# An attention and MLP backward kernel bound by its DMA: head 0's scores ahead of the output-gradient columns, the first loads reordered, dx sums and a weight load moved forward

## The chip, the cores and the metric

The kernel runs on one core of one Trainium2 chip. The metric is device time in microseconds (us), the median over executions. A core has a matrix engine (PE; its weight loads are listed as PEld), a vector engine (DVE), a scalar engine (ACT), GpSimd (POOL) and SyncE (SP, which here issues loads and, at the very end, two tiny stores). In the timelines below each engine takes its instructions in the order in which the program lists them, so that one whose inputs are ready can stand behind others. The profile counts sixteen DMA engines; a DMA share of 1.00 means that all sixteen are busy.

## The reference, cut to what matters

The result is the output of a gated mix of one attention step and one MLP, and the gradients of nine inputs. There is one query token, 32 heads, a K and a V cache of 4096 x 128 bf16 (1 MB each) per head, and a model width of 640.

```python
def _fwd_reference(A_x, A_k_cache, A_v_cache, A_wq, A_wo, B_x, B_w1, B_b1, B_w2, gate_w):
    x = A_x                                           # (1, 1, 640)
    g = _sigmoid((x * gate_w).sum(-1, keepdims=True))
    a = _A_ref(x, A_k_cache, A_v_cache, A_wq, A_wo)   # q = x@wq; softmax(q.K)V; @ wo
    b = _B_ref(B_x, B_w1, B_b1, B_w2)                 # 640 -> 1728 -> 640
    return g * a + (1 - g) * b

def reference(..., grad_out):
    _out, _vjp = jax.vjp(_f, A_x, A_k_cache, A_v_cache, A_wq, A_wo, B_w1, B_b1, B_w2, gate_w)
    return (_out, *_vjp(grad_out))
```

For each head the kernel reads K and V and writes gradients dK and dV of the same size: 32 heads times four tiles of 1024 KB are 134 MB of the 164.93 MB that it moves. The weights and their gradients are the rest.

## The kernel before

Everything is unrolled in Python. Heads come in groups of four (G = 4). One load of Wq serves eight heads (1280 KB), one load of Wo four (640 KB). All large loads go through SP's queue, in this order at the start:

```python
vec_rows = const.tile([3 * RC, P], BF16, name="vec_rows")
nc.scalar.dma_start(vec_rows[0:RC, :], x_rows)            # three tiny loads, by ACT
nc.scalar.dma_start(vec_rows[RC:2 * RC, :], dy_rows)
nc.scalar.dma_start(vec_rows[2 * RC:3 * RC, :], gw_rows)
...
load_wq(0); load_wo(0); load_k(0); load_v(0); load_k(1); load_v(1); load_wo(1)
# w1_sb, b1c
load_k(2); load_v(2)
load_w2(0); load_w2(1)         # two tiles w2c of 96 partitions x 7680 bytes, 720 KB each
```

Gradients dK and dV go out by GpSimd's queue as each head ends. `products` are matrix-vector products on transposed chunks of K or V; `qd` holds the columns of q and of the output gradient that they are multiplied with. These columns are prepared group by group. Small pieces of work (`steps`) wait in a list, and `slot` issues those whose inputs were issued in an earlier slot:

```python
add(n("qcol"), "P", qcol, (), head)                       # q = Wq x, needs the Wq load
add(n("doa"), "D", do_part(0, 2), (), head)               # output gradient, needs Wo
add(n("dob"), "D", do_part(2, 4), (n("doa"),), head)
add(n("qbc"), "P", qbc, (n("qcol"),), head)
add(n("dbc"), "P", dbc, (n("dob"), n("qbc")), head)
add(n("dcol"), "P", dcol, (n("dbc"),), head)
add(n("m2"), "T", m2, (n("dcol"),), head)                 # columns of q AND gradient
add(n("x2"), "P", x2, (n("m2"),), head)
```

```python
prep_steps(0, 0)
for _ in range(8):
    slot(0, 9, 9)              # all of head 0's columns first
tk = []
for c in range(NT):            # then head 0's scores
    k_chunk(0, c, tk)
    if c:
        s_chunk(0, c - 1, tk)
s_chunk(0, NT - 1, tk)
mlp_steps()
for h in range(H):
    hh, g = h % G, h // G
    if hh == 3:
        load_wo(g + 2)
        if g % 2 == 0:
            load_wq(g // 2 + 1)      # reuses the tile that the dx sums read
    load_k(h + 3)
    load_v(h + 3)
    if hh == 1 and g + 1 < NG:
        rest = steps[:]
        steps.clear()
        prep_steps(g + 1, h)         # the next group's columns go first
        steps.extend(rest)
    ...
    period(h)                        # softmax, dP, dV, dq, next head's scores, store of dV
```

(Cuts are marked by dots; assertions are left out.)

## Time and profile before

| | before |
|---|---|
| median, range (first 3 runs) | 413.43 us, 413.16 to 413.49 |
| span of the profiled run | 412.1 us |
| moved by DMA | 164.93 MB, mean 400 GB/s |
| busy: DVE, PE, ACT | 75%, 74%, 43% |
| first store of dV issued | 29.66 us |

A kernel that moves 164.93 MB at the 421 GB/s of most of its span needs 392 us, so about 20 us are to be found where the rate is lower. The page's second part cuts the span into 40 equal slices. Its line DMA gives the mean busy share of the sixteen engines in tenths; the line GB/s gives what they moved. Before:

```profile
DMA  8999999999999999999999999999999999999970
GB/s 292 421 405 336 421 425 415 421 423 425 420 426 422 423 411 415 424 421 422 427 411 425 423 421 419 420 424 393 407 401 428 422 422 421 422 423 383 421 313 14
DMA packets 26328, 164.93 MB, mean 400 GB/s; under 512 B 2812, under 2 KB 2812, under 8 KB 10012
```

The slice that reads 336 (30.9 to 41.2 us) is remarkable: the engines are as busy as elsewhere and move less. The view of windows gives, for each stretch, its start, end and length in us, then busy us and number of instructions of PE, PEld, DVE, ACT and POOL, then the granted PE clock, the DMA share and GB/s. Before:

```profile
0.00:4.00 4.00, 0.00 (x0) 0.00 (x0) 1.45 (x7) 1.28 (x1) 0.94 (x11) 1.00 0.46 134
4.00:16.00 12.00, 3.73 (x40) 2.64 (x40) 5.41 (x22) 2.18 (x7) 0.00 (x0) 1.00 1.02 407
30.00:36.00 6.00, 5.01 (x112) 4.62 (x110) 4.48 (x11) 3.24 (x8) 0.85 (x2) 1.00 1.01 244
30.00:40.00 10.00, 7.74 (x142) 6.95 (x141) 7.88 (x19) 4.57 (x11) 0.93 (x3) 0.92 1.01 315
270.00:290.00 20.00, 13.82 (x251) 12.64 (x252) 12.56 (x32) 7.18 (x17) 1.59 (x3) 0.73 0.99 406
400.00:407.00 7.00, 0.00 (x0) 0.00 (x0) 0.00 (x0) 0.00 (x0) 0.00 (x0) 0.50 0.06 26
```

From 30 to 36 us the rate is 244 GB/s at a DMA share of 1.01: this is "the dip" from here on. What ran there is in the DMA view of 30 to 35 us, before (queue, packets, MB, share of the sixteen engines; q1 carries the loads that SP issues, q0 the transfers that GpSimd issues):

```profile
DMA packets 179, 1.23 MB, mean 245 GB/s; under 512 B 21, under 2 KB 21, under 8 KB 172
## 3 DMA queue, kind: packets, MB, share of 16 engines
q1 hardware_dynamic: 178, 1.21, 100.0%
```

Only loads are in flight, and nearly all their packets are under 8 KB: these are the 7680-byte rows of w2c. They take 503 ns each here (median of the packet records of the two tiles), but 291 ns at 208 to 226 us, where stores run beside the same sort of load. Loads without stores are not slow as such: just before, K and V load alone (99% of the engines' time) at 415 GB/s and 309 ns for an 8 KB packet:

```profile
26.00:29.00 3.00, 2.47 (x45) 2.12 (x42) 2.68 (x7) 1.21 (x3) 0.00 (x0) 1.00 0.99 415
```

Nor is it the row of 7680 bytes alone: the six 8 KB packets that start at 30 to 35 us take 456 to 541 ns too. So every load packet beside w2c is slow while no store runs; what makes it so is not shown. No store runs at 30 to 35 us because the first one has only just been issued, as the timeline of before shows (start, length, engine, line, operation, in brackets how long the engine had been idle and what ended it):

```profile
6.74 0.17 PE L180 MATMUL cols_ps<-ident_bf,vec_rows 15*128 15x15 bf16 x1 [6.74 <-DMA vec_rows<-in_gate_w_dram]
11.25 0.67 PE L269 MATMUL qc_ps<-cols_bf,wq_g 128*128 128x1 bf16 x20
16.77 1.95 PE L559 MATMUL tr<-ident_f,Kn 128*128 128x128 f32 x8
22.29 0.19 DVE L632 TENSOR_REDUCE m<-sA 128x1 f32<-128x32 f32 x1 [5.60 <-PE sA L568]
29.66 0.67 POOL L611 DMA_DIRECT2D out_dram<-dV_sb  x1 [28.10 <-DVE o_all L673]
```

The tiny vectors land at 6.7 us, q is made at 11.25, the transposes of K0 start at 16.77 after the gradient columns, the scores end on PE at 22.25, and the store of dV is issued at 29.66. At the end of the kernel, 26 GB/s from 400 to 407 us is one sixteenth of 421: one engine finishes late.

### The profile page before, as it was taken

The page shows a single profiled execution, that of the slowest core. Times are in us where ns is not written, and L with a number is a line of the kernel's source. Part 1 is how long each engine was busy: PE and PEld are TensorE (multiplying, and loading weights), DVE is VectorE, ACT ScalarE, POOL GpSimd, SP SyncE. Part 2 cuts the span into 40 slices and gives each one's busy share as a digit, 9 for nine tenths or more (in the row PEclk, how much of TensorE's full clock was granted, in tenths as well). Part 3 has the DMA queues.
Part 4 walks back from the last instruction along what each step waited for, and adds up shares of the span by engine and source line. Part 5 has one row for each costly group of instructions (what it writes and reads, how often), then busy time and mean ns, then how long its engine had stood idle before and what let it go on. Part 6 is the DMA issues. An engine that isn't in the chain of part 4 may idle for free.

```text
span 412.1 us, 13687 instructions
## 1 busy us (share of the span) xinstructions
PE 305.7 (74%) x5916; PEld 277.5 (67%) x5916; DVE 308.8 (75%) x807; ACT 177.0 (43%) x410; POOL 49.9 (12%) x95
## 2 busy tenths in 40 slices
PE   0688899988998789898977688439888788886200
PEld 0577888888887678787867687428777678775200
DVE  3338655685679999999897688528999997978840
ACT  1354534434445455445534356305554555543000
POOL 0001001111110111121111112001111111133310
PEclk9998999999999999989996899958999999999555
DMA  8999999999999999999999999999999999999970
GB/s 292 421 405 336 421 425 415 421 423 425 420 426 422 423 411 415 424 421 422 427 411 425 423 421 419 420 424 393 407 401 428 422 422 421 422 423 383 421 313 14
DMA packets 26328, 164.93 MB, mean 400 GB/s; under 512 B 2812, under 2 KB 2812, under 8 KB 10012
## 3 DMA queue, kind: packets, MB, share of 16 engines
q1 hardware_dynamic: 14116, 82.03, 48.8%
q0 software_dynamic: 12112, 82.03, 47.8%
q8 instruction: 46, 0.75, 0.7%
q14 instruction: 14, 0.11, 0.1%
q10 hardware_dynamic: 40, 0.01, 0.0%
HBM read 82.03 MB, written 82.03 MB: 398 GB/s over the span
## 4 chain that ended last, share of the span: by engine, by line
DVE 33%; PE 30%; DMA 23%; ACT 7%; issue 3%; ACTq 0%; DVEq 0%
DMA Kn<-in_A_k_cache_dram 17%; PE tr L559 10%; DVE dK_sb L584 8%; DVE dV_sb L584 7%; DMA out_dram<-dK_sb 6%; ACT tT L561 6%; PE sA L628 4%; DVE junk L376 4%; PE sA L568 3%; PE h_ps L407 3%; PE sB L681 3%; DVE junk L279 2%; DVE junk L508 2%; PE sB L568 1%; DMA vec_rows<-in_gate_w_dram 1%
## 5 line engine op out<-in xcount | busy, mean ns | idle before, releaser
L561 ACT COPY tT<-tr 128x512 f32<-128x512 f32 x256 | 142.3, 587 | 140.9 <-PE tr L559 140.2
L568 PEld LDWEIGHTS <-tT 128*128 128x128 bf16 x2048 | 80.4, 98 | 40.3 <-ACT tT L561 34.9
L559 PE MATMUL tr<-ident_f,Kn 128*128 128x128 f32 x512 | 80.7, 295 | 6.5 <-DMA Kn<-in_A_k_cache_dram 6.5
L584 DVE TENSOR_TENSOR dV_sb<-p_bf,qd 128x2048 bf16<-128x2048 bf16 x64 | 77.9, 1218 | 2.8 <-DMA out_dram<-dK_sb 2.8
L584 DVE TENSOR_TENSOR dK_sb<-ds_bf,qd 128x2048 bf16<-128x2048 bf16 x64 | 77.7, 1215 | 0.0
L559 PE MATMUL tr<-ident_f,Vn 128*128 128x128 f32 x512 | 72.6, 277 | 0.1
L568 PE MATMUL sA<-qd,tT 128*128 128x48 bf16 x1024 | 48.8, 187 | 23.5 <-ACT dq_all L686 12.8
L559 PEld LDWEIGHTS tr<-ident_f,Kn 128*128 128x128 f32 x512 | 60.1, 150 | 7.6 <-issue 6.2
L559 PEld LDWEIGHTS tr<-ident_f,Vn 128*128 128x128 f32 x512 | 56.8, 143 | 0.2 <-PE sA L568 0.2
L568 PE MATMUL sB<-qd,tT 128*128 128x48 bf16 x1024 | 46.1, 183 | 0.1
L611 POOL DMA_DIRECT2D out_dram<-dV_sb x32 | 18.3, 572 | 166.8 <-DVE dV_sb L584 74.2
L628 PEld LDWEIGHTS <-Vn 128*128 128x128 bf16 x1024 | 30.2, 96 | 10.4 <-issue 10.4
L601 POOL DMA_DIRECT2D out_dram<-dK_sb x31 | 18.3, 591 | 151.0 <-DVE rz L650 77.7
L628 PE MATMUL sA<-e_bf,Vn 128*128 128x48 bf16 x1024 | 30.7, 183 | 7.6 <-DVE zs L648 6.0
L681 PE MATMUL sB<-ds_bf,Kn 128*128 128x48 bf16 x1024 | 31.8, 185 | 3.5 <-DVE ds_bf L670 3.5
L681 PEld LDWEIGHTS <-Kn 128*128 128x128 bf16 x1024 | 29.2, 97 | 3.8 <-issue 3.8
L632 DVE TENSOR_REDUCE m<-sA 128x1 f32<-128x32 f32 x32 | 6.0, 189 | 31.3 <-PE sA L568 25.6
L279 DVE SCALAR_TENSOR_TENSOR junk<-wo_g,da_bc 128x640 bf16<-128x640 bf16 x32 | 26.3, 821 | 2.6 <-ACT da_bc L220 1.1
L376 DVE SCALAR_TENSOR_TENSOR junk<-wq_g,dq_bc 128x1024 bf16<-128x1024 bf16 (+1 forms) x25 | 25.1, 1004 | 0.2
L668 DVE TENSOR_SCALAR_CACHE_REDUCE dj<-sB,rz 128x128 f32<-128x128 f32 x32 | 11.1, 346 | 11.2 <-PE sB L662 11.2
L407 PE MATMUL h_ps<-cols_bf,w_sb 128*96 128x1 bf16 x90 | 18.2, 313 | 1.4 <-ACT qd L290 0.7
L407 PEld LDWEIGHTS <-w_sb 128*96 128x96 bf16 x90 | 17.6, 272 | 1.8 <-issue 0.7
(144 smaller groups left out, 283.8 us busy)
## 6 DMA issues: line engine op xcount, KB each, us to landing
Kn<-in_A_k_cache_dram SPq DMA_DIRECT2D x32, 1024.0 KB, 27.2
Vn<-in_A_v_cache_dram SPq DMA_DIRECT2D x32, 1024.0 KB, 26.9
out_dram<-dV_sb POOLq DMA_DIRECT2D x32, 1024.0 KB, 12.2
out_dram<-dK_sb POOLq DMA_DIRECT2D x31, 1024.0 KB, 12.3
wq_g<-in_A_wq_dram SPq DMA_DIRECT2D x4, 1280.0 KB, 19.0
wo_g<-in_A_wo_dram SPq DMA_DIRECT2D x8, 640.0 KB, 13.3
out_dram<-wo_g POOLq DMA_DIRECT2D x8, 640.0 KB, 11.6
out_dram<-dwq_t POOLq DMA_DIRECT2D x5, 896.0 KB, 16.6
```

The costliest lines, as they stand in the source:

```text
L279: nc.vector.scalar_tensor_tensor(junk[:, 0:D], in0=wos[g][:, i, :], scalar=1.0, in1=da_bc[:], op0=ALU.mult, op1=ALU.mult, accum_out=gp["do ...
L376: nc.vector.scalar_tensor_tensor(junk[:, c0:c1], in0=wqs[w][:, rc, c0:c1], scalar=1.0, in1=dq_bc[:, w * WG * Dh + c0:w * WG * Dh + c1], op ...
L407: nc.tensor.matmul(hps[a][:, fc:fc + 1], lhsT=w1_sb[:, rc, :].rearrange("p (q c) -> p q c", c=FCN)[:, :, fc], rhs=x_bf[:, rc:rc + 1], star ...
L559: nc.tensor.transpose(tp[:, t, :], flat[:, k * P:(k + 1) * P], ident_f[:])
L561: nc.scalar.copy(sb[:].rearrange("p a b -> p (a b)"), tp[:].rearrange("p a b -> p (a b)"))
L568: nc.tensor.matmul(out[:, 2 * k:2 * k + W], lhsT=tb[:, t, par, :], rhs=vec[:, par, :].unsqueeze(1).to_broadcast([P, W // 2, 2]), start=(pa ...
L584: nc.vector.tensor_tensor(dst[:, a:b, :].rearrange("p j (a b) -> p j a b", b=2), col[:, a:b, :].unsqueeze(2).to_broadcast([P, n, Dh // 2, 2]),
L601: nc.gpsimd.dma_start(dKv[h], st["dK"][:])
L611: nc.gpsimd.dma_start(dVv[h], st["dV"][:])
L628: nc.tensor.matmul(O, lhsT=vts[h][:, j, :], rhs=st["e"][:, j:j + 1].to_broadcast([P, W]), start=(j == 0), stop=(j == J - 1))
L668: nc.vector.tensor_scalar(dj[:], PT, rz[:], None, ALU.mult, ALU.add, accum_out=dd[:])
L681: nc.tensor.matmul(DQ, lhsT=kts[h][:, j, :], rhs=ds[:, j, 0:1].to_broadcast([P, W]), start=(j == 0), stop=(j == J - 1))
```

## The change

The intent is to make head 0 start, and so store, earlier. The scores need only q and K0, so q's columns are prepared apart from those of the output gradient. The vectors that q needs are loaded first, on SP; the first Wq goes by GpSimd's queue at the same time; K0 comes ahead of Wo. In the middle, the sums for dWo and dx go ahead of the next group's preparation (`first=True`), and Wq is loaded one head earlier.

```diff
-    nc.scalar.dma_start(vec_rows[0:RC, :], x_rows)
+    nc.sync.dma_start(vec_rows[0:RC, :], x_rows)          # and dy_rows, gw_rows
...
-            nc.sync.dma_start(wqs[w][:], wq_v[...])
+            (nc.sync if w else nc.gpsimd).dma_start(wqs[w][:], wq_v[...])
...
     load_wq(0)
+    load_k(0)
     load_wo(0)
-    load_k(0)
...
         add(n("qcol"), "P", qcol, (), head)
+        add(n("m2q"), "T", m2(0), (n("qcol"),), head)
+        add(n("x2q"), "P", x2(0), (n("m2q"),), head)
...
-        add(n("m2"), "T", m2, (n("dcol"),), head)
-        add(n("x2"), "P", x2, (n("m2"),), head)
+        add(n("m2d"), "T", m2(1), (n("dcol"),), head)
+        add(n("x2d"), "P", x2(1), (n("m2d"),), head)
...
-        add(n("dwo"), "D", dwo, (n("aadd"),))             # dx likewise
+        add(n("dwo"), "D", dwo, (n("aadd"),), first=True)
...
-    for _ in range(8):
-        slot(0, 9, 9)
     tk = []
-    for c in range(NT):
-        k_chunk(0, c, tk)
-        if c:
-            s_chunk(0, c - 1, tk)
+    slot(0, 1, 1)
+    k_chunk(0, 0, tk)
+    slot(0, 1, 1)
+    k_chunk(0, 1, tk)
+    slot(0, 1, 1)
+    for c in range(1, NT):
+        if c > 1:
+            k_chunk(0, c, tk)
+        s_chunk(0, c - 1, tk)
     s_chunk(0, NT - 1, tk)
+    while steps:
+        slot(0, 9, 9)
...
+        if hh == 2 and g % 2 == 0:
+            load_wq(g // 2 + 1)
         if hh == 3:
             load_wo(g + 2)
-            if g % 2 == 0:
-                load_wq(g // 2 + 1)
...
-            rest = steps[:]
-            steps.clear()
+            ahead = [st for st in steps if st[5]]         # those with first=True
+            rest = [st for st in steps if not st[5]]
+            steps[:] = ahead
```

More of the change, by code (lines that the diff above doesn't have):

```diff
@@ L107 @@
     vec_rows = const.tile([3 * RC, P], BF16, name="vec_rows")
-    nc.scalar.dma_start(vec_rows[0:RC, :], x_rows)
-    nc.scalar.dma_start(vec_rows[RC:2 * RC, :], dy_rows)
-    nc.scalar.dma_start(vec_rows[2 * RC:3 * RC, :], gw_rows)
+    nc.sync.dma_start(vec_rows[0:RC, :], x_rows)
+    nc.sync.dma_start(vec_rows[RC:2 * RC, :], dy_rows)
+    nc.sync.dma_start(vec_rows[2 * RC:3 * RC, :], gw_rows)
     kts, vts, wqs, wos = {}, {}, {}, {}
@@ L126, in load_wq @@
             wqs[w] = wts.tile([P, RC, WG * Dh], BF16, name="wq_g", tag="wq_g")
-            nc.sync.dma_start(wqs[w][:], wq_v[:, :, w * WG * Dh:(w + 1) * WG * Dh])
+            (nc.sync if w else nc.gpsimd).dma_start(wqs[w][:], wq_v[:, :, w * WG * Dh:(w + 1) * WG * Dh])
     def load_wo(g):
@@ L238, with add @@
     steps, done = [], {}
-    def add(name, kind, fn, deps=(), head=0):
-        steps.append((name, kind, fn, tuple(deps), head))
+    def add(name, kind, fn, deps=(), head=0, first=False):
+        steps.append((name, kind, fn, tuple(deps), head, first))
     slot_no = [0]
@@ L250, in slot @@
             for st in list(steps):
-                name, k, fn, deps, head = st
+                name, k, fn, deps, head, _ = st
                 if k != kind or head > h or not room[k]:
@@ L301, in dcol, with m2, f, x2 @@
                                  rhs=ident_bf[:, 0:1], start=True, stop=True)
-        def m2():
-            gp["m2"] = small.tile([P, 2, G, 2], BF16, name="m2", tag="m2")
-            for w, src in ((0, gp["qc"]), (1, gp["dc"])):
+        def m2(w):
+            def f():
+                if w == 0:
+                    gp["m2"] = small.tile([P, 2, G, 2], BF16, name="m2", tag="m2")
+                src = gp["dc"] if w else gp["qc"]
                 nc.vector.tensor_tensor(gp["m2"][:, w], src[:].unsqueeze(2).to_broadcast([P, G, 2]),
                                         mask2[:].to_broadcast([P, G, 2]), ALU.mult)
-        def x2():
-            x2 = gr_ps.tile([P, 2, G, 2], F32, name="x2_ps", tag="gr")
-            nc.tensor.matmul(x2[:].rearrange("p a b c -> p (a b c)"), lhsT=sel2[:],
-                             rhs=gp["m2"][:].rearrange("p a b c -> p (a b c)"), start=True, stop=True)
-            t = gp["x2"] = qds[g % 3]
-            hf = P // 2
-            nc.scalar.mul(t[0:hf, :, :, :, 0], x2[0:hf], scale)
-            nc.scalar.mul(t[hf:P, :, :, :, 1], x2[hf:P], scale)
+            return f
+        def x2(w):
+            def f():
+                x2 = gr_ps.tile([P, G, 2], F32, name="x2_ps", tag="gr")
+                nc.tensor.matmul(x2[:].rearrange("p b c -> p (b c)"), lhsT=sel2[:],
+                                 rhs=gp["m2"][:, w].rearrange("p b c -> p (b c)"), start=True, stop=True)
+                t = gp["x2"] = qds[g % 3]
+                hf = P // 2
+                nc.scalar.mul(t[0:hf, w, :, :, 0], x2[0:hf], scale)
+                nc.scalar.mul(t[hf:P, w, :, :, 1], x2[hf:P], scale)
+                gp[f"x{w}"] = True
+            return f
         n = lambda x: f"{x}{g}"
         add(n("qcol"), "P", qcol, (), head)
+        add(n("m2q"), "T", m2(0), (n("qcol"),), head)
+        add(n("x2q"), "P", x2(0), (n("m2q"),), head)
         add(n("doa"), "D", do_part(0, 2), (), head)
@@ L392, in finish_steps @@
             elif g % 2 == 1:
-                add(n(f"dx{rc}_"), "D", dx(rc, 0, WG * Dh, g // 2), (n("dqb"),))
+                add(n(f"dx{rc}_"), "D", dx(rc, 0, WG * Dh, g // 2), (n("dqb"),), first=True)
     def mlp_steps():
@@ L578, in s_chunk @@
             sts[h] = {"A": sa_ps.tile([P, 512], F32, name="sA", tag="sA")}
+        assert gp["x0"]
         products(sts[h]["A"][:, 0:J + W], ts[c], c, gp["x2"][:, 0, h % G])
@@ L620, in period @@
         DP, DQ, PT = B[:, 0:J + W], B[:, 128:128 + W], B[:, 256:384]
+        assert gp["x1"]
         vec = gp["x2"][:, 1, h % G]
@@ L706 @@
     prep_steps(0, 0)
-    for _ in range(8):
-        slot(0, 9, 9)
-    tk = []
-    for c in range(NT):
-        k_chunk(0, c, tk)
-        if c:
-            s_chunk(0, c - 1, tk)
-    s_chunk(0, NT - 1, tk)
+    tk = []
+    slot(0, 1, 1)
[7 more added lines that the diff above has]
+        s_chunk(0, c - 1, tk)
+    s_chunk(0, NT - 1, tk)
+    while steps:
+        slot(0, 9, 9)
     mlp_steps()
@@ L717 @@
         hh, g = h % G, h // G
+        if hh == 2 and g % 2 == 0:
+            assert g == 0 or f"dx{RC - 1}_{g - 1}" in done
+            load_wq(g // 2 + 1)
         if hh == 3:
@@ L720 @@
             load_wo(g + 2)
-            if g % 2 == 0:
-                assert g == 0 or f"dx{RC - 1}_{g - 1}" in done
-                load_wq(g // 2 + 1)
         load_k(h + 3)
```

## The prediction

> **What bounds the kernel.** The DMA, nearly everywhere. The page shows 164.93 MB moved in a 412.1 us span; in the table of 4 us windows almost every window stands at 415 to 430 GB/s with a DMA share of 1.0, while DVE is busy 75%, PE 74%. At 421 GB/s the bytes alone take 392 us. The other 20 us are: the start (134 GB/s in 0-4 us, 378 in 4-8: about 3 us lost); a dip at 30-36 us (about 245 GB/s although the share reads 1.0: about 2.5 us lost); weaker dips at 280-304 and 374-377 (about 2 us); and the tail. From 400 to 407 us the DMA view shows 26 GB/s, a sixteenth of full rate: one of the 16 engines is still working when the others have finished (about 399.7). The last loads show the same lag: from 358 to 369 the load queue trickles. The Trainium skill, "DMA: Bandwidth & Descriptors", section "Latency and other measured facts", says that some engines are usually slower; the trace agrees (about 8 us late), without naming which. So the end is set by the slowest engine's total work, hardly by compute. The last arithmetic, 0.25 us on ACT, ends at 397, before the last stores.
>
> **What the change does.** Same bytes, same mathematics. Three tiny vector loads go first on SP: now they land at 6.6 us (behind the weights), then at an estimated 3. The first Wq goes through the GpSimd queue, which shares the engines with K0. There is a risk: the first GpSimd store took 6 us from issue (29.66) to its first packet, later ones 1.3 to 4; so Wq may land at 8.5 to 12.5 (6.9 now). Scores need only q and K0; today they wait for output-gradient columns: transposes start at 16.8, scores end at 22.2 (5.4 us). Afterwards I expect scores at 14 to 18 and head 0's first dV store issued at 23 to 26 instead of 29.66. Added: one m2 (0.17 us) and one x2 group (0.5 us) per group of heads, eight times, hidden. dwo and dx ahead of the next group's preparation, and Wq loaded one head earlier, shorten waits on the SP queue (63 us waiting for wo_g stores), but in those stretches the DMA is saturated already.
>
> **What of it counts.** Four to six us of compute lead early are mostly absorbed: head 4's K is throttled by bandwidth, and by 264-274 compute idles for K anyway. The real gain is the dip: 30-36 us is the two 720 KB w2c loads running alone, 1.47 MB in 6 us; the same sort of load beside stores (208-214 us) runs with 405 GB/s in total. Earlier stores overlap it: about 2 us saved of 2.5. On the other side, SP's bulk stream starts up to 1 us later behind three 0.3 to 0.56 us issues, partly covered by Wq. Middle and tail: about 0.
>
> **Predicted: 411.5 us, range 408.7 to 413.8.** Faster by over 2%: 0.03; within 2%: 0.95; slower by over 2%: 0.02.
>
> **What would show it right.** First DMA_DIRECT2D store of dV at 23-26 us; no stretch near 245 GB/s at 30-36; scores of head 0 before the output-gradient columns, ended by 18 us; GB/s elsewhere 420; the one-engine tail still there, about 8 us.
>
> **What would make it wrong.** Wq landing after 13 us (dip stays: 413 to 414); a slower start; or the one late engine having slack in the middle, idle at the waits for wo_g stores, which the earlier dwo and Wq would fill: then 405 to 408. Delayed preparation stalling group boundaries would cost 1 to 3.

## The result and the profile after

The changed kernel takes 416.12 us (median of four runs, 415.99 to 416.97), the kernel before 413.46 (four runs, 413.16 to 413.77). Ratios in this document are the mean time of one kernel's runs over that of the kernel before in the same rounds, so they are not quite the ratio of the medians: here 1.0069, with a 95% interval of 1.0051 to 1.0086. That is within 2%, but it is a loss of nearly 3 us, where a gain of 2 was predicted, and it lies outside the predicted range. The record marks the results of all experiments as correct.

The page after, same lines as above:

```profile
DMA  7999999999999999999999999999999999999970
GB/s 269 400 422 318 422 416 421 427 422 425 424 421 423 418 420 426 422 421 424 421 420 424 423 420 423 425 382 329 416 419 423 424 420 403 424 420 418 420 317 14
DMA packets 26008, 164.93 MB, mean 398 GB/s; under 512 B 2812, under 2 KB 2812, under 8 KB 9692
```

The bytes are the same. The rate is lower in the first two slices (269 and 400, against 292 and 421), the dip is still there (318 against 336; over 30 to 40 us 313 against 315), and there is a new hole in the slices that read 382 and 329, at 269 to 290 us. The windows after:

```profile
0.00:4.00 4.00, 0.17 (x1) 0.10 (x1) 1.25 (x7) 1.46 (x2) 1.97 (x12) 1.00 0.28 73
4.00:16.00 12.00, 2.65 (x33) 2.13 (x34) 3.64 (x18) 1.22 (x4) 0.00 (x0) 1.00 1.00 389
30.00:40.00 10.00, 7.63 (x177) 7.25 (x178) 7.41 (x19) 4.61 (x12) 1.13 (x2) 1.00 1.02 313
270.00:290.00 20.00, 17.09 (x368) 15.67 (x367) 15.66 (x40) 11.82 (x27) 2.14 (x4) 0.95 0.92 352
403.00:410.00 7.00, 0.00 (x0) 0.00 (x0) 0.00 (x0) 0.00 (x0) 0.00 (x0) 0.50 0.06 24
```

Summed over the packet records, after is 1.1 us of bytes (at 421 GB/s) behind before by 16 us and 3.0 us behind by 296 us. The loss is made by then, in these stretches, and the one-engine tail has only moved along. At 264 us it is only 0.6 us behind, so in bytes most of the gap opens at 270 to 290. Bytes that are behind in the middle aren't time lost one to one, however, and the experiments below weigh the two stretches otherwise. Why the start went wrong is in the timeline after:

```profile
1.29 1.00 POOL L127 DMA_DIRECT2D wq_g<-in_A_wq_dram  x1 [0.84 <-POOLq L820]
3.26 0.17 PE L180 MATMUL cols_ps<-ident_bf,vec_rows 15*128 15x15 bf16 x1 [3.26 <-DVE ident_bf L166]
15.04 0.69 PE L269 MATMUL qc_ps<-cols_bf,wq_g 128*128 128x1 bf16 x20 [6.82 <-DMA wq_g<-in_A_wq_dram]
17.77 0.17 DVE L283 CAST do4b<-do 128x4 bf16<-128x4 f32 x1
22.57 0.52 PE L103 MATMUL d_ps<-ident_bf,do4b 128*128 128x128 bf16 x4
24.14 0.18 DVE L642 TENSOR_REDUCE m<-sA 128x1 f32<-128x32 f32 x1
31.86 0.58 POOL L620 DMA_DIRECT2D out_dram<-dV_sb  x1 [28.73 <-DVE o_all L683]
```

The vectors are there by 3.3 us, as intended. But Wq, issued at 1.29, is there only at 15.04; before, it had landed at 6.9. From that point on head 0 is later than before: the scores end on PE at 22.74 (DVE reads them at 24.14, because the gradient columns stand ahead in its order), and the first dV store comes at 31.86 in place of 29.66. Wq's first packets run at 4.9 us. The DMA view after, from 5.4 us to 14.9, shows what it was doing:

```profile
q1 hardware_dynamic: 384, 2.36, 63.3%
q0 software_dynamic: 325, 1.27, 36.4%
```

Wq (on q0) has 36% of the engines and the bulk loads of SP have 63%. The Trainium skill, "DMA: Bandwidth & Descriptors", section "Issuing engines are not separate DMA queues", says that transfers issued by different engines run on the same sixteen DMA engines and interleave. The trace agrees: a second issuing engine bought no bandwidth, it only took Wq out of its place at the head of the line. Its packets are 4 KB and K's are 8 KB in the packet records, which fits with its smaller share.

The timeline shows a second delay: `do4b`, from which the gradient columns are made, is ready at 17.9, but its broadcast `d_ps` starts at 22.57, because in PE's order it now stands behind all of head 0's scores. And the sums of the output gradient are split by the wait for q: two of the four stand in DVE's order behind the new `m2q`, which waits for Wq.

The waits of PE over the span (waiting instruction, what it waited for, us in total, times, longest), before:

```profile
PE qc_ps L269 <- DMA wq_g<-in_A_wq_dram: 11.5, 1, 11.5
PE tr L559 <- DMA Kn<-in_A_k_cache_dram: 6.5, 3, 2.9
```

and after:

```profile
PE tr L567 <- DMA Kn<-in_A_k_cache_dram: 17.3, 3, 13.2
PE qc_ps L269 <- DMA wq_g<-in_A_wq_dram: 6.8, 1, 6.8
```

So there is a wait of 13.2 us for one K tile, which ends at 266.6 us, just before the hole of 270 to 290 us. It has taken the place of another: in the kernel before, PE waited 11.5 us for the last Wq, until 274.1. From 225 to 290 us PE waits for loads 15.4 us in sum before and 14.8 after, so the hole isn't explained by more waiting. (The 6.8 us of after is the first Wq, at the start.)

### The profile page after: what moved, and what is told of

It reads as the page before. It is cut to its first block, busy times and chain, and to the rows that moved or that the text cites. A ratio compares the mean times of both kernels' runs of the same rounds, so it can differ in the third digit from the quotient of the medians.

```text
span 414.3 us, 13720 instructions
## 1 busy us (share of the span) xinstructions
PE 306.8 (74%) x5924; PEld 278.7 (67%) x5924; DVE 308.2 (74%) x807; ACT 179.0 (43%) x426; POOL 50.9 (12%) x96
## 4 chain that ended last, share of the span: by engine, by line
DVE 35%; PE 29%; DMA 20%; ACT 8%; issue 4%; ACTq 0%; DVEq 0%; POOLq 0%
DMA Kn<-in_A_k_cache_dram 17%; PE tr L567 10%; DVE dK_sb L593 9%; DVE dV_sb L593 7%; ACT tT L569 7%; PE sA L638 4%; PE sA L576 4%; DVE junk L384 4%; PE sB L691 3%; DMA wq_g<-in_A_wq_dram 3%; PE h_ps L415 3%; DVE junk L279 3%; DVE junk L516 2%; DVE wo_g L373 2%; DVE zs L658 1%
## 5 line engine op out<-in xcount | busy, mean ns | idle before, releaser
L576 PEld LDWEIGHTS <-tT 128*128 128x128 bf16 x2048 | 79.7, 98 | 42.3 <-ACT tT L569 35.4
L567 PE MATMUL tr<-ident_f,Kn 128*128 128x128 f32 x512 | 81.6, 296 | 17.3 <-DMA Kn<-in_A_k_cache_dram 17.3
L567 PEld LDWEIGHTS tr<-ident_f,Kn 128*128 128x128 f32 x512 | 61.0, 151 | 17.8 <-issue 17.8
L576 PE MATMUL sA<-qd,tT 128*128 128x48 bf16 x1024 | 48.7, 187 | 24.4 <-ACT tT L569 12.7
L415 PEld LDWEIGHTS <-w_sb 128*96 128x96 bf16 x90 | 17.6, 272 | 1.7 <-issue 0.7
L662 ACT ACTIVATE p_bf<-e_bf,rz 128x64 bf16<-128x64 bf16 x32 | 11.1, 348 | 13.9 <-DVE rz L660 11.9
## 6 DMA issues: line engine op xcount, KB each, us to landing
Vn<-in_A_v_cache_dram SPq DMA_DIRECT2D x32, 1024.0 KB, 26.3
out_dram<-dV_sb POOLq DMA_DIRECT2D x32, 1024.0 KB, 11.9
out_dram<-dwq_t POOLq DMA_DIRECT2D x5, 896.0 KB, 15.8
```

The source lines that it names most:

```text
L415: nc.tensor.matmul(hps[a][:, fc:fc + 1], lhsT=w1_sb[:, rc, :].rearrange("p (q c) -> p q c", c=FCN)[:, :, fc], rhs=x_bf[:, rc:rc + 1], star ...
L567: nc.tensor.transpose(tp[:, t, :], flat[:, k * P:(k + 1) * P], ident_f[:])
L576: nc.tensor.matmul(out[:, 2 * k:2 * k + W], lhsT=tb[:, t, par, :], rhs=vec[:, par, :].unsqueeze(1).to_broadcast([P, W // 2, 2]), start=(pa ...
L662: nc.scalar.activation(p_bf[:], e[:].unsqueeze(2).to_broadcast([P, J, 2]), ACT.Copy, scale=rz[:])
```

## The experiments

The theory after reading the two traces was: the loss is mostly made at the start, by Wq's late landing through GpSimd's queue (theory 1). Its rivals: the bulk stream starts later behind the vectors, and that alone is the loss (theory 2); the loss is made in the middle, by the reordered sums or the early Wq (theory 3). Beside these stood the question whether the dip costs what the prediction said it costs. "dV" below is the issue of the first dV store, in us, in the profiled run.

### Start and middle apart, and the dip alone

`start_only` is the changed kernel with the middle put back:

```diff
-        if hh == 2 and g % 2 == 0:  load_wq(g // 2 + 1)
+        if hh == 3 and g % 2 == 0:  load_wq(g // 2 + 1)
-            ahead = [...]; rest = [...]; steps[:] = ahead
+            rest = steps[:]; steps.clear()
```

> The changed kernel with its middle part undone (Wq loaded at the fourth head of a pair again, dwo and dx no longer ahead of the next preparation); the start of the change stays. Theory A, the start alone costs it (Wq by the GpSimd queue lands at 15 us instead of 6.9, head 0 begins 1.8 us later, the bytes moved by 16 us are 1.1 us behind): 415.5 to 416.5, as the changed kernel. Theory B, the stall at 264 to 296 us costs most of it (2 us of bytes lost there): 413.5 to 414.5.

`mid_only` is the changed kernel with the start put back (the split into q and gradient columns stays, but the scores wait for all columns, as before):

```diff
-    (changed order of vectors, first Wq, K0)
+    (order of the kernel before)
-    slot(0, 1, 1); k_chunk(0, 0, tk); slot(0, 1, 1); ...
+    while steps: slot(0, 9, 9)
+    (all of k_chunk and s_chunk)
```

> The middle part alone, with the split columns it needs; loads and order of the start as in the kernel before. Theory A: 413 to 413.7, as before. Theory B: 415 to 416. If both parts cost by themselves and add up: about 414.5 here and 415 in start_only.

`wq_on_sp` is the changed kernel with the first Wq back on SP, behind the vectors:

```diff
-            (nc.sync if w else nc.gpsimd).dma_start(wqs[w][:], ...)
+            nc.sync.dma_start(wqs[w][:], ...)
```

> The changed kernel with only the first Wq back on the SP queue, behind the three small vectors and ahead of K0. Theory A: Wq lands by 7 to 8 us, scores of head 0 end by 15, first dV store issued at 23 to 26 (31.9 in the changed kernel), part of the w2c dip is covered; 411.5 to 413.5. Theory B: the start improves but the stall near 264 to 296 stays: 414 to 415.5.

`w2_late` is the kernel before with the two w2c loads moved into the loop of the heads, where stores run beside them:

```diff
-    load_w2(0)
-    load_w2(1)
...
+        if h == 2:
+            load_w2(0)
+            load_w2(1)
         load_k(h + 3)
```

> The kernel before with the two first w2c loads issued two heads later, beside stores. If the 245 GB/s of 30 to 36 us come from w2c loads running alone and cost the end of the kernel, the dip goes and 411 to 412 results (2 us less than before). Rival: the end is set by one late engine or by stalls later, which make up for the dip: 413 to 414, though the dip is gone.

| | ratio (95%) | median us | dV |
|---|---|---|---|
| start_only | 1.0046 (1.0034 to 1.0058) | 415.98 | 33.51 |
| mid_only | 1.0020 (1.0008 to 1.0032) | 414.78 | 29.31 |
| wq_on_sp | 1.0006 (0.9991 to 1.0021) | 414.24 | 30.18 |
| w2_late | 0.9959 (0.9946 to 0.9972) | 412.42 | 29.61 |

The two halves add up: 0.46% and 0.20% are 0.66%, and the whole change costs 0.69%. So theory 1 and theory 3 each hold a part. With Wq on SP about 0.6% is gone, although the rest of the change is all there. Its first store came at 30.18, not at 23 to 26 as expected: this profile is of the slowest of its six runs, and although its scores ended at 18.7, PE ran at half pace until 26.3 (more on this pace below). And the dip is worth what the prediction had said: with w2c loaded later, the stretch from 30 to 40 us runs at full rate. Window of w2_late, same columns as above:

```profile
30.00:40.00 10.00, 8.82 (x192) 8.17 (x191) 8.45 (x21) 5.34 (x13) 1.33 (x3) 1.00 1.01 418
```

At 418 for 315 GB/s over 10 us, this stretch alone moves 1.03 MB more, 2.4 us at 421 GB/s. The kernel gains 0.41% of 414 us, 1.7 us: by the packet records 0.9 us of the lead is lost again between 48 and 64 us, where w2c now runs.

The moved tiles are the same two, and in `w2_late` their packets take 291 ns, at 45 to 57 us with stores beside them (53% of the engines' time), against 503 ns before. `w2_late` is faster than both kernels.

### Which part of the start

`vec_on_act` goes one step further than `wq_on_sp` and puts the vectors back on ACT too. What then remains of the change at the start is K0 ahead of Wo, the split, and the new order of the scores:

```diff
 (wq_on_sp, and)
-    nc.sync.dma_start(vec_rows[0:RC, :], x_rows)       # and the other two
+    nc.scalar.dma_start(vec_rows[0:RC, :], x_rows)
```

> The changed kernel with the first Wq on SP and the three small vectors back on ACT; K0 before wo0, early scores and the middle part stay. Theory S, the three small issues ahead of the bulk on SP are what put the bytes 1.05 us back by 16 us (as in the run with Wq alone back on SP): bytes by 16 us as before, and 1 us less than that run, ratio 0.998 to 0.9995. Rival: the bytes come late for another reason, or the lateness is absorbed: ratio 1.000 to 1.002.

`wq_pool_only` is the kernel before with nothing changed but the first Wq on GpSimd:

```diff
-            nc.sync.dma_start(wqs[w][:], ...)
+            (nc.sync if w else nc.gpsimd).dma_start(wqs[w][:], ...)
```

> The kernel before with nothing changed but the first Wq issued by the GpSimd queue. Theory: Wq lands at 13 to 15 us instead of 6.9, scores of head 0 end at 24 to 25.5 instead of 22.2, the first dV store is issued 2 to 3 us later, so the w2c loads run alone for 1 to 1.5 us longer: ratio 1.0015 to 1.003, with the bytes by 16 us as before. Rival: the start of head 0 is off the bound, ratio 1.000.

`first_only` tests the middle: it is `mid_only` with Wq back at hh == 3, so that only the reordered sums are left:

```diff
 (mid_only, and)
-        if hh == 2 and g % 2 == 0:  load_wq(g // 2 + 1)
+        if hh == 3 and g % 2 == 0:  load_wq(g // 2 + 1)
```

> The middle part without its earlier Wq load: dwo and dx ahead of the preparation, split columns, start as before. Theory M1, the early Wq load (640 packets of 2 KB ahead of K) makes K wait 43 us and starves the DMA at 270 to 290: here that wait is back at 33 us, bytes there at 385 GB/s or more, ratio 1.000. Theory M2, the order of the steps does it: 360 and 340 GB/s at 270 to 290 as with the whole middle part, ratio 1.002.

`after_w2_late` asks whether the loss of the changed kernel goes away when w2c is loaded late. It is the changed kernel with the edit of `w2_late`.

> The changed kernel with the first two w2c loads issued two heads later. If its loss is made of a longer dip (about 1 us), late bulk loads (1 us) and the middle (0.8 us), and the dip goes here: ratio 1.000 to 1.002 to the kernel before, 2 to 3 us less than the changed kernel. If the GpSimd Wq costs by another way than the dip, it stays at 1.004 or more.

| | ratio (95%) | median us | dV |
|---|---|---|---|
| vec_on_act | 0.9988 (0.9973 to 1.0002) | 412.94 | 26.57 |
| wq_pool_only | 1.0040 (1.0025 to 1.0055) | 415.53 | 33.42 |
| first_only | 1.0006 (0.9994 to 1.0018) | 414.27 | 29.55 |
| after_w2_late | 1.0052 (1.0040 to 1.0064) | 416.04 | 31.65 |

One line, GpSimd for SP at the first Wq, costs the kernel before 0.40% (more than the 0.15 to 0.30% that had been expected), nearly all that the start of the change costs. Wq then lands 15.8 us after its issue, and the scores end at 26.0 us instead of 22.3. In bytes nothing is lost by 36 us (0.1 us); 0.8 us is lost between 36 and 40, where the dip lasts longer. This settles theory 1 for the start.

Theory 2 has a small part. By 16 us `wq_on_sp` is 1.05 us of bytes behind the kernel before, `vec_on_act` 0.06: the three vector issues ahead of the bulk cost 1 us of transfer. The window of 0 to 4 us shows it, in wq_on_sp:

```profile
0.00:4.00 4.00, 0.29 (x2) 0.26 (x2) 1.79 (x10) 1.46 (x2) 0.94 (x11) 1.00 0.25 40
```

and in vec_on_act:

```profile
0.00:4.00 4.00, 0.00 (x0) 0.00 (x0) 1.45 (x7) 1.28 (x1) 0.94 (x11) 1.00 0.47 132
```

In time the two differ by 0.18%, with intervals that overlap, so that this microsecond is shown in bytes and only likely in time.

`vec_on_act` is also the version that does what the change was meant to do: dV at 26.57, three microseconds early, and the dip mostly gone (this profile is of the fastest of its six runs). Window of vec_on_act:

```profile
30.00:40.00 10.00, 8.76 (x187) 7.89 (x187) 9.52 (x25) 5.88 (x16) 1.06 (x2) 1.00 1.01 398
```

Two later kernels with the same start and w2c in its old place give steps between: `w3_late` stored dV at 27.82 and moved 362 GB/s at 30 to 40 us, `best_a` 28.04 and 345, the kernel before 29.66 and 315. So the mechanism of the predicted gain is real: an earlier first store does fill the dip. The changed kernel only failed to have an earlier first store.

`after_w2_late` is a miss that teaches something. The dip at 30 to 40 us is gone (422 GB/s), but the time is not: w2c has moved behind the second Wq, and loads run nearly alone once more, at 54 to 56 and 60 to 64 us (227 and 301 GB/s). Window of after_w2_late:

```profile
56.00:64.00 8.00, 7.64 (x140) 7.22 (x138) 5.28 (x16) 4.25 (x9) 1.07 (x2) 1.00 1.00 351
```

From the packet records it is 1.4 us of bytes ahead of before at 48 us and 1.1 us behind at 64.

### Looking for the best version, and for the role of K

`best_a` is `vec_on_act` with the middle put back; `best_b` is `best_a` with w2c late; `wq_act_queue` is `best_b` with the later Wq loads on ACT's queue, so that K needn't stand behind them:

```diff
 best_a:  (vec_on_act, and)  load_wq at hh == 3; rest = steps[:]; steps.clear()
 best_b:  (best_a, and)      load_w2(0); load_w2(1) at h == 2
 wq_act_queue: (best_b, and)
-            nc.sync.dma_start(wqs[w][:], ...)
+            (nc.scalar if w else nc.sync).dma_start(wqs[w][:], ...)
```

> Early scores alone with a good start: vectors on ACT, Wq on SP first, K0 second, columns split; the middle as before. If early scores were right and only their loads were wrong: first dV store at 26 to 27 us, no 245 GB/s stretch, and without the 0.2% of the middle part ratio 0.996 to 0.998. Rival, a lead of head 0 is worth nothing at the end: 0.9995 to 1.0005.

> The same with the first two w2c loads two heads later as well. Both cures act on the same dip of 2.5 us, so they should not add: ratio 0.995 to 0.997, near the 0.9959 of the later w2c loads alone. If a lead of head 0 had a worth of its own: 0.993 to 0.9945.

> The last one with the three later Wq loads issued from the ACT queue, so that K and V loads need not stand behind 640 packets of 2 KB in the SP queue. If the waits for K in the middle (33 us from issue to landing, compute idle for 10 us) cost time: ratio 0.002 to 0.005 below the last one. If the DMA is full there anyway, as the prediction held: the same within 0.001.

`wq_pool_w2_late` asks whether a late head 0 costs anything once there is no dip. It is `wq_pool_only` with w2c late.

> The first Wq by the GpSimd queue and the first two w2c loads two heads later, else the kernel before. If the 0.4% that Wq costs by the GpSimd queue pass through a longer lonely w2c stretch, they vanish with it: ratio 0.996 to 0.998. If Wq costs them otherwise: 1.000, that is 0.4% above the later w2c loads alone.

| | ratio (95%) | median us | dV |
|---|---|---|---|
| best_a | 0.9966 (0.9946 to 0.9987) | 412.32 | 28.04 |
| best_b | 0.9959 (0.9944 to 0.9974) | 412.10 | 28.06 |
| wq_act_queue | 0.9974 (0.9959 to 0.9989) | 412.69 | 26.59 |
| wq_pool_w2_late | 1.0003 (0.9991 to 1.0015) | 414.32 | 32.91 |

The two cures of the dip don't add: `best_b` is as fast as `w2_late` with its one moved pair of lines. The waits of `wq_act_queue` show none of PE for a K tile (6.5 us in `best_b`), and nothing is gained. But the test is mixed: its stretch from 50 to 60 us is down to 350 GB/s, and 1.75 us of its lead in bytes is lost between 40 and 64 us. At 64 us it is 0.6 us ahead of the kernel before, and at 360 again, so that the missing waits bring nothing that can be seen.

`wq_pool_w2_late` was a surprise. It has hardly a dip (389 GB/s at 30 to 40 us), but next to `w2_late`, from which it differs in one line, it loses 0.44%. By the packet records its bytes are 1.5 us ahead of before until 128 us, and behind by 160. The windows of w2_late in this stretch:

```profile
128.00:136.00 8.00, 6.21 (x119) 5.61 (x116) 7.90 (x24) 4.26 (x10) 1.06 (x2) 1.00 1.01 424
136.00:144.00 8.00, 6.46 (x150) 5.81 (x148) 7.69 (x23) 4.14 (x11) 1.07 (x2) 1.00 1.01 423
152.00:160.00 8.00, 7.29 (x180) 6.81 (x178) 7.59 (x22) 4.11 (x10) 1.06 (x2) 1.00 1.02 417
```

and of wq_pool_w2_late:

```profile
128.00:136.00 8.00, 7.07 (x171) 6.49 (x172) 7.89 (x20) 4.12 (x10) 0.89 (x2) 1.00 1.01 398
136.00:144.00 8.00, 5.92 (x126) 5.29 (x123) 7.89 (x22) 3.87 (x10) 1.24 (x3) 1.00 0.98 373
152.00:160.00 8.00, 6.75 (x184) 6.38 (x184) 7.59 (x22) 2.68 (x7) 1.07 (x2) 1.00 1.02 381
```

DVE is busy 7.6 to 7.9 of every 8 us in both: there the arithmetic of DVE sets the pace, and the chain of waits has only compute in this stretch. The compute that started late can't catch up there, loads are released late, and the load queue runs dry: from 149.2 to 152.2 us its packets take 3% of the engines' time (60% in `w2_late`). Over the three windows the difference is (26 + 50 + 36) GB/s times 8 us, 0.9 MB, or 2.1 us. So a late head 0 has a second price, paid at 130 to 160 us, but only by a kernel whose DMA has run ahead. `wq_pool_only`, with head 0 as late and the dip in place, is 1.2 us behind before at 128 us and at 160, and the changed kernel itself moves 413 to 424 GB/s from 128 to 160: neither pays it.

### The middle: the last Wq load

`w3_late` and `after_w3_late` put only the last Wq load back to hh == 3, in `vec_on_act` and in the changed kernel. `w3_w2_late` is `w3_late` with w2c late.

```diff
-        if hh == 2 and g % 2 == 0:
+        if hh == (2 if g < 4 else 3) and g % 2 == 0:
```

> The changed kernel with vectors on ACT and the first Wq on SP (0.9988 before), and of the three later Wq loads only the last one a head later again, as in the kernel before. If it is that one load, at 219 us instead of 242, that leaves the DMA dry at 270 to 290 (370 to 390 GB/s there): no such loss, ratio 0.9945 to 0.9965. If the earlier dwo and dx or the split columns cost it: 0.998 to 0.9995 again.

> The changed kernel itself (1.0069) with only that last Wq load a head later again. If the late part of its loss is that load: 1.002 to 1.004 and 385 GB/s or more at 270 to 290. If not: 1.006 to 1.007.

> The first run of this call with the first two w2c loads two heads later: head 0 early, no lonely w2c stretch, Wq early but for the last. If these add, 0.993 to 0.996, the fastest so far. If the lead of head 0 has taken the stretch away already: as the first run of this call within 0.001.

| | ratio (95%) | GB/s at 270 to 290 us | longest wait of PE for K, 225 to 290 us |
|---|---|---|---|
| before | 1 | 406 | 2.9 us |
| first_only | 1.0006 | 395 | 2.7 us |
| start_only | 1.0046 | 408 | 3.2 us |
| mid_only | 1.0020 | 353 | 13.2 us |
| after | 1.0069 | 352 | 13.2 us |
| after_w3_late | 1.0049 (1.0037 to 1.0061) | 386 | 2.3 us |
| vec_on_act | 0.9988 | 382 | 11.9 us |
| w3_late | 0.9984 (0.9968 to 1.0001) | 384 | 2.7 us |
| w3_w2_late | 1.0014 (1.0002 to 1.0026) | 385 | 2.5 us |

The cause of the long K wait is settled: a K wait of 10.7 to 13.2 us stands in all five kernels that load the last Wq early and were profiled (after, mid_only, wq_on_sp, vec_on_act and after_w2_late) and in none of the others. The kernels with the last Wq at hh == 3 have a wait of PE for that Wq in its place (11.5 us before, 7.3 in after_w3_late, 8.9 in w3_late). The last Wq was issued at 219.7 us in after, ahead of a K tile issued at 224.1, which the chain of waits shows 42.4 us on its way; before, Wq was issued at 242.4, behind the store of a wo_g tile that SP waited for. There is another trace of the early load. SP's own waits, after:

```profile
SPq L127 <- DVE junk L384: 15.5, 2, 9.4
```

Here SP, which issues in order, waits for the dx sums that still read the old Wq tile, with the K and V loads behind it. The kernels with Wq at hh == 3 have no wait of this kind of half a microsecond or more.

What this costs in time is less clear. Three pairs say that the middle costs some 0.2%: mid_only alone (0.20%), after against start_only (0.23%), vec_on_act against best_a (0.22%). In the changed kernel, moving the last Wq back brings 0.20%; in `vec_on_act` it brings 0.04% and no rate, though the K wait goes away there too. The intervals overlap, and both runs fell outside what had been expected of this load (0.9945 to 0.9965 for w3_late, 1.002 to 1.004 for after_w3_late). So the early last Wq load probably is the middle's loss in the changed kernel, and the reordered sums cost no more than 0.18% (first_only), but the runs don't settle the sizes. `w3_w2_late`, meant as a sum of gains, lost its gain at 56 to 64 us (328 GB/s), where w2c again ran behind an additional Wq load, as in `after_w2_late`.

### Repeat of the best, and a try to steady PE's early pace

The first dV store came at 26.57 to 29.75 us in profiles of kernels with the same start code. Most of that goes with PE's pace. Transposes of K0 in vec_on_act (four in each line):

```profile
11.80 1.09 PE L567 MATMUL tr<-ident_f,Kn 128*128 128x128 f32 x4
15.22 0.64 PE L567 MATMUL tr<-ident_f,Kn 128*128 128x128 f32 x4
```

and in w3_w2_late, which has the same start:

```profile
15.37 1.10 PE L565 MATMUL tr<-ident_f,Kn 128*128 128x128 f32 x4
22.49 1.06 PE L565 MATMUL tr<-ident_f,Vn 128*128 128x128 f32 x4
```

The pace nearly doubles at 14 us in one and at about 24 in the other. In the six kernels with this start the clock records put the doubling at 13.8 (vec_on_act), 14.0 (wq_act_queue), 17.9 (w3_late), 18.9 (best_b), 19.0 (best_a) and 24.4 us (w3_w2_late), and the first dV store at 26.57, 26.59, 27.82, 28.06, 28.04 and 29.75: the later the one, the later the other. The code doesn't set this moment, so that a single profile's dV, and how far it fills the dip, are partly luck. (The clock column of the windows is no guide here: before, it reads 1.00 at 16 to 20 us, where four transposes take 1.09 us; the first clock record is at 21.2.) The Trainium skill, "TensorE: Matmul & The Clock Gate", section "Part 1: The HAM clock gate (the "warmup" mystery)", describes this: PE runs at half its clock until it has been busy through a window of about 3.4 us, and the window runs free of the kernel. The two paces (1.09 and 0.64 us) and the varying moment agree with it. So `warm_best_b` and `warm_w2_late` add 25 transposes into a scratch tile while PE has nothing else to do:

```diff
+    warm(16)     # 16 transposes of ident_f into a scratch tile
     nc.tensor.transpose(cols_ps[:], vec_rows[:], ident_bf[0:3 * RC, 0:3 * RC])
...
     nc.tensor.transpose(z_ps[:], z1[:].to_broadcast([P, P]), ident_f[:])
+    warm(9)
```

> The good start with later w2c loads (0.9959 before), and 25 idle-time transposes on PE, 16 ahead of the vectors' columns and 9 in the gap after them, so that PE has been busy before head 0. Theory: the same start code stored head 0's dV first at 26.6 to 29.8 us in five profiles, because four transposes take 1.09 us until PE's pace doubles, at another moment in each run. Then here: 0.64 us for four from the second chunk at the latest, first dV store at 25.5 to 26.6, a spread of the timed runs under 1.5 us (2.4 so far), ratio 0.993 to 0.9955. Rival, the pace is fixed by something else: four transposes still take 1.09 us, ratio 0.9959 as before.

> The later w2c loads alone (0.9959 and 0.9952), with the same 25 transposes. If the lead of head 0 still has a worth once the lonely w2c stretch is gone: first dV store at 27 to 28 instead of 29.3 to 29.6, ratio 0.993 to 0.995. If not: 0.995 to 0.996.

`w2_late_again` is `w2_late` without any change, to see whether its gain stands.

> The later w2c loads alone, again, on the chip of the others, so that the fastest version can be named: 0.9945 to 0.9972 as the first time.

| | ratio (95%) | median us | dV |
|---|---|---|---|
| warm_best_b | 0.9973 (0.9943 to 1.0002) | 412.21 | 29.49 |
| warm_w2_late | 0.9952 (0.9940 to 0.9964) | 411.95 | 29.78 |
| w2_late_again | 0.9952 (0.9940 to 0.9964) | 411.99 | 29.34 |

The warm-up failed. In `warm_w2_late` the clock records show full speed from 4.5 to 7.9 us and from 11.3 to 14.7, half speed after each, and full speed for good from 21.6; in `warm_best_b` full speed came at 23.3. The stores came no earlier. The gain of `w2_late` stands: 0.48% in the repeat, 2.0 us. It beats both kernels, and nothing built on top of it was measurably faster.

## Why the prediction was wrong, and where it was right

- **"Wq may land at 8.5 to 12.5" was the step that failed.** It landed at 15.0. The prediction had named both the delay of GpSimd's first packet and the sharing with K0. The delay was within what it had allowed: 3.6 us from issue to the first packets (it had seen 1.3 to 6). The sharing was the term that it mis-sized: issue at 1.3 and 6 us of delay leave 5.2 us for the transfer in its latest case (12.5), which is what Wq takes alone at the head of SP's queue (1.9 to 6.9 us before), so that, by this estimate from the prediction's own numbers, next to nothing was allowed for K0. With 36% of the engines' time the transfer took 10.1 us (4.9 to 15.0). The prediction's own list of what would make it wrong has this case ("Wq landing after 13 us (dip stays: 413 to 414)"), with the price too low: the start costs 0.46%, 1.9 us, against the kernel before.
- **"Scores at 14 to 18 and head 0's first dV store issued at 23 to 26" failed with it.** The scores ended on PE at 22.7 and the store came at 31.86. With Wq on SP and the vectors on ACT the scores did end at 17.6 (`vec_on_act`), as predicted, but the store came at 26.57 at best. Two things held it that the prediction had left out: PE is at half pace early on, until a moment that differs from run to run, and the gradient columns stand behind the scores in PE's order, which in the changed kernel put 1.6 us between the end of the scores on PE (22.7) and the first transpose of V (24.3), and 1.4 us in `vec_on_act` (17.6 to 19.0).
- **"About 2 us saved of 2.5" for the dip was right in size, but not had.** `w2_late` removes the dip and gains 1.7 and 2.0 us; `vec_on_act`, with an earlier store, fills it from 315 to 398 GB/s in its profile.
- **"SP's bulk stream starts up to 1 us later, partly covered by Wq" was right in its first half.** The stream was 1.05 us behind by 16 us (`wq_on_sp`), and 0.06 when the vectors were on ACT again. Nothing covered it: Wq's first packets ran at 4.9 us, too late to fill in.
- **"Four to six us of compute lead early are mostly absorbed" doesn't hold for a lag in every kernel.** `wq_pool_w2_late`, whose DMA had run ahead, showed a stretch at 128 to 160 us where DVE is busy about 95%; what started late there lets the DMA run dry, for 2.1 us. The changed kernel lost nothing there, so that this is no part of its loss.
- **"Middle and tail: about 0" was mis-sized for the middle.** It measured 0.20% or 0.8 us, with a K wait of up to 13.2 us, shown to come from the last Wq load's earlier place. The prediction's "by 264-274 compute idles for K anyway" was a misreading: there the kernel before waits 11.5 us for the last Wq, the very load that the change moves. The move exchanged one wait for another; why the DMA has a hole after the second (352 against 406 GB/s at 270 to 290 us) and what it costs wasn't settled.
- **The tail was right.** One engine's rate (26 GB/s before, 24 after) stands in both for the last 7 us, only 3 us later. The Trainium skill, "DMA: Bandwidth & Descriptors", section "Latency and other measured facts", says that two of the engines are usually slower than the others; the trace agrees that one ends about 8 us late, without a name. What makes it late is open.
- The feared cost at group boundaries and the hoped-for slack of the late engine didn't show: `first_only` is at 1.0006 (0.9994 to 1.0018).

## What to carry to other kernels

In this kernel, moving a load to another issuing engine didn't give it more bandwidth, because the DMA was the limit: it took the load out of its place in the order. The load that everything waits for should be first in one queue, with nothing beside it. A stretch with a full DMA share and a low rate should be looked at for which transfers run in it; here, moving two loads to where stores run beside them gained more than all the reordering of compute. And a full DMA on average doesn't mean that compute's lead is free to be spent: look for the stretch in which an engine is busy all the time, for that is where a late start can be paid. Before a wait is called new, the waits of the kernel before should be listed too: it may only have changed its name. And a moment taken from a single profile can owe more to the clock of that run than to the code.

## What the Trainium skill lacked or had wrong

- "DMA: Bandwidth & Descriptors", section "Specifications", gives a first-byte latency of about 1 us for transfers issued by GpSimd. Here the first Wq's first packets ran 3.6 us after its issue began (1.29 to 4.9 us), and those of the first dV store of the kernel before 5.8 us after (29.66 to 35.4).
- The same page says that engines share the DMA but gives no figure for what a load loses when it is taken from the head of one queue to a queue of its own: 1280 KB landed 13.7 us after its issue beside K0, against 6.2 us at the head of SP's queue.
- No page says how fast tiles of 96 partitions with rows of 7680 bytes load: 245 GB/s when they run alone, with all engines busy (503 ns for a packet), and full rate beside stores (291 ns). K and V loads alone (99% of the engines' time, at 26 to 29 us in the kernel before) ran at 415 GB/s. The cause is open.
- No page gives the price of small loads ahead of a bulk stream on the same queue: 1 us of bytes for three. They landed by 3 us on SP, and by 6.7 us on ACT behind the bulk.
- "TensorE: Matmul & The Clock Gate", section "Part 1: The HAM clock gate (the "warmup" mystery)", has the two paces right, and the return to half speed after an idle window: in `warm_w2_late` PE was nearly idle from 5 to 8 us, and full speed ended at 7.9. But about 3.4 us of sustained work didn't always bring full speed: in `warm_best_b` PE is listed as busy for 6.29 of the 6.3 us from 7.9 to 14.2, and it came at 23.3. Listed as busy is not the same as at its peak, so that what the clock counts as work stays open.
